# First MLP product of the last three chunks from seven block products instead of eight, on one Trainium2 core

## The chip, the core and the metric

The kernel runs on one core of a Trainium2 chip. The metric is the device time of one execution in microseconds (us), median of the runs of a kernel. The profile names the engines: PE is TensorE (matrix products) and PEld its weight loads, DVE is VectorE, ACT is ScalarE, POOL is GpSimd, SP is SyncE, which issues transfers.

## The reference, cut to what matters

An attention over four batches of 768 rows is followed by a Fourier mixing and a normalised MLP. The change touches the MLP's first product alone.

```
attn = softmax(scores with a global/local mask and a distance bias) @ v     # 4 batches, 8 heads, 768 x 64
x = attn, heads joined                                                      # [4, 768, 512]
u = x + real(fft(fft(x, axis=1), axis=2))
un = (u - mean) / sqrt(var + 1e-06)
out = u + maximum(un @ w_ch1, 0) @ w_ch2                                    # w_ch1 [512, 2048], w_ch2 [2048, 512]
```

## The kernel before, in words

**Tiling.** The MLP works on twelve chunks of 256 rows, three per batch, so that chunks 9, 10 and 11 are those of the last batch. A chunk has two halves of 128 rows. `un` is brought to the layout `UNT[c]` (features on the partitions) by a transposing transfer (`nt_dma`, issued by SP). The first product, `un @ w_ch1`, is made by `ph_unit(c, jp)`, eight units per chunk: a unit is 8 matmuls of 128x128 weights against 256 columns (2 of the 16 blocks of hidden features, 4 blocks of input features each), and one evacuation of a 128x512 PSUM bank with the relu to the tile `hT`, on ACT (L1344) or DVE (L1345). The second product is in `pg_units(c)`. For chunks 2 to 11 it is already made from seven block products in place of eight: units p1, p45, p6, p7, p32, with sums of `hT` blocks made on DVE (`s_sums`: s1, s2, s3, s4) and sums of `w_ch2` blocks made once (`w2_sums`). Each p unit ends in a DVE operation that adds the product, scaled, to `u` (L1502).

**Order.** Nothing is scheduled at run time. Every operation is registered with a name, and `ORDER` lists for each engine the names in the order in which it issues them; each engine works strictly in that order. A planner made the lists from its own costs (functions `mm_us`, `act`, `dve`, `dve2`, `pool`) and a rule for DVE operations that run beside POOL copies (`beside`, `SLOW`). A name is the unit and the operation's number in it: `H72.0` is the first operation behind PE unit H72.

Names that the steps below use:

- PE: `H8c`..`H8c+7` are the units of chunk c's first product. `G` are the units of the second: chunk 6 is G36 to G40, chunk 7 G41 to G45, chunk 8 G46 to G50, chunk 9 G51 to G55, chunk 10 G56 to G60, chunk 11 G61 to G66. `A64` is a score unit and `A73` to `A76` are the four products of the last batch's attention weights with v. M27, M28, M30, M31 are the last batch's Fourier products `py`, M29 and M32 the products `pu` that give u for chunks 9 and 10 (M29) and 11 (M32).
- DVE: T.191 to T.196 are the folds ahead of M27 and M28 (T.191 is L907 and L908). T.220 is s4 of chunk 5; T.224, T.225, T.227 are s1, s2, s3 of chunk 6; T.241 and T.242 are s1 and s2 of chunk 9; T.247 to T.250 belong to chunk 10, T.252 to T.255 to chunk 11. M29.0, M29.6 and M32.0 add `pu` to x for chunks 9, 10 and 11. T.197 is the copy of a mirrored block (L1139 to L1141) that M32 reads.
- POOL: M23.11, M26.5, M29.5 ... are the two small operations (L1285, L1286) that make 1/std of a chunk; T.190 gathers x of the last batch; T.234 and T.251 store chunks 7 and 10 by an indirect transfer (L1355).
- SP: T.189 reads x of the last batch; T.198 to T.200 are the transposing transfers of chunks 9 to 11; T.222 and T.223 store chunk 5, T.228 and T.229 chunk 6, T.239 and T.240 chunk 8, T.256 to T.258 chunk 11 in three pieces.

PSUM has eight banks: two pairs in the ring `xx` (scores, attention products, Fourier products), two banks in `ph`, two in `pg`. The attention weights stand in four tiles `ex0` to `ex3` (`expst`), which the last batch leaves free after A73 to A76.

Of the kernel before, what the change touches and what calls it, by code (L numbers as in the profile page):

```python
# [24 lines left out]
class Plan:  # L25
# [96 lines left out]
    def op_go(self, eng, name, start):  # L122
# [6 lines left out]
        if eng == "POOL":  # L129
            self.ports.append((start, end, 1 if dma else 0 if outs and outs[0][0] in ("vB", "kB") else 2))  # L130
# [23 lines left out]
    SLOW = ((0.56, 1.0, 1.0), (0.38, 0.7, 1.0))  # L154
    ports = ()

    def beside(self, start, cost, kind):

        left, t = cost, start
        names = self.todo["POOL"]  # L160
        ports = self.ports[-3:]
        if names:
            s = self.op_start("POOL", names[-1])
            if s is not None:
                p = self.made[names[-1]]
                ports = ports + [(max(s, start), max(s, start) + p[0]["POOL"][0], 1 if p[7] else 0 if p[3] and p[3][0][0] in ("vB", "kB") else 2)]
        for a, b, dma in ports:
            if b <= t:
                continue
            if a > t:  # L170
                if a - t >= left:
                    break
                left -= a - t
                t = a
            rate = self.SLOW[kind][dma]
            if (b - t) * rate >= left:
                return t + left / rate - start
            left -= (b - t) * rate
            t = b
        return t + left - start  # L180
# [40 lines left out]
    def unit_start(self, unit):  # L221
# [7 lines left out]
        if not there:  # L229
# [33 lines left out]
        ),  # L263
        "DVE": (
# [11 lines left out]
        ),  # L276
        "POOL": (
# [8 lines left out]
            "T.140 T.205 T.212 T.206 T.186 T.211 T.149 T.179 T.180 T.150 T.151 T.229 T.189 T.228 T.223 T.222 T.198 T.199 T.200 T.240 T.239 T.245 T.246 "  # L286
            "T.256 T.258 T.257 "
# [73 lines left out]
def kernel(  # L361
# [986 lines left out]

    GP = {}
# [125 lines left out]
    def pg_units(c):  # L1475
# [104 lines left out]
        PG.append((h0 + wd + [("D",)], ("pg",), p1))  # L1580
        PG.append((h1 + [("s", c, 1)] + ws, ("pg",), p45))
# [31 lines left out]
    with tc.manual_schedule():  # L1613
# [76 lines left out]
        for b in range(B):  # L1690
# [49 lines left out]
            nt_unit(b, 2)  # L1740
        for c in range(NP * B):
            for jp in range(NJ // 2):
                ph_unit(c, jp)
# [7 lines left out]
        for i in range(2):  # L1751
            w2_sums(i)
        pl.run([MIX, ATT, PH, PG])
# [35 lines left out]
```

## Time and profile before

| what | value |
|---|---|
| time, median of 3 runs | 245.82 us (245.44 to 248.03) |
| span of the profiled execution, first to last instruction | 244.1 us |
| median less span (what lies around the span; the profile does not give the execution's own time beside its span) | 1.7 us |
| PE busy | 232.0 us, 95% |
| DVE, ACT, POOL busy | 193.4, 138.8, 114.8 us |

How to read it: an engine's busy time is the union of its instructions. The chain that ended last follows the work back from the last instruction; the line that stands there for a stretch is what set the time in it. A row of the time line gives the start, the duration, the engine, the line of the kernel, and out<-in. Where a row merges several instructions, the duration is that of them all. A PE row ends some 0.17 us after the next one has begun, since matmuls are pipelined; the pace is read from start to start. DVE and ACT rows overlap in the same way by about 0.1 us.

### The profile page before, as it was taken

What the parts mean: (1) busy time and instruction counts of PE and PEld (TensorE: products, weight loads), DVE (VectorE), ACT (ScalarE), POOL (GpSimd) and SP (SyncE); (2) the same over time, 40 slices, a digit from 0 to 9 for tenths busy, and PEclk for the clock granted to TensorE, in tenths of its full rate; (3) what the DMA queues carried; (4) which work ended last, traced back from release to release, by engine and by line L of the source; (5) the groups of instructions that cost most, each with busy time, mean ns of one, the idle gap of its engine ahead of it and who ended that gap; (6) DMA issues with size and microseconds to landing.
All of it is one profiled execution on the core that took longest, in us unless ns stands there. A gap on an engine that the chain in (4) does not pass through costs nothing.

```text
span 244.1 us, 7606 instructions
## 1 busy us (share of the span) xinstructions
PE 232.0 (95%) x3251; PEld 191.2 (78%) x3251; DVE 193.4 (79%) x420; ACT 138.8 (57%) x226; POOL 114.8 (47%) x164
## 2 busy tenths in 40 slices
PE   7679899999999999999999999999999999999993
PEld 2557776878677667788989888898889898888883
DVE  2559997879972789999999889889998755846483
ACT  2368788864657468658357788364534651434200
POOL 8998898866590038999059056500300320011020
PEclk9997999999999999999999999999999999999999
DMA  6999999999999999999999979220570330040212
GB/s 170 181 169 145 157 235 172 197 190 196 110 145 152 234 179 205 117 135 110 242 184 285 135 84 156 46 33 13 174 258 4 77 99 0 1 130 1 89 72 99
DMA packets 95938, 32.85 MB, mean 135 GB/s; under 512 B 84160, under 2 KB 92480, under 8 KB 95904
## 3 DMA queue, kind: packets, MB, share of 16 engines
q0 software_dynamic: 66176, 17.06, 71.7%
q1 hardware_dynamic: 26560, 12.56, 25.1%
q10 hardware_dynamic: 3168, 2.75, 4.1%
q8 instruction: 25, 0.41, 0.7%
q14 instruction: 9, 0.07, 0.1%
HBM read 31.44 MB, written 8.65 MB: 164 GB/s over the span
## 4 chain that ended last, share of the span: by engine, by line
PE 67%; DMA 14%; DVE 5%; ACT 5%; POOL 3%; issue 3%; SPq 1%; POOLq 0%
PE ph L1339 29%; PE pgD L1484 14%; PE pgA L1484 10%; DMA qk<-in_q_dram 4%; DMA v<-in_v_dram 4%; PE py L1105 3%; DMA hT<-in_q_dram 3%; PE pg L1370 3%; PE pav L822 3%; ACT ex L766 2%; DMA back<-backm 2%; DMA xr<-xd,back 2%; PE sc L737 2%; PE pu L1192 1%; ACT mk L1657 1%
## 5 line engine op out<-in xcount | busy, mean ns | idle before, releaser
L1339 PE MATMUL ph<-unT,w 128*128 128x256 f16 x768 | 94.4, 273 | 0.8 <-issue 0.4
L1339 PEld LDWEIGHTS <-w 128*128 128x128 f16 x768 | 73.6, 98 | 12.5 <-issue 1.2
L1344 ACT ACTIVATE hT<-ph 128x512 f16<-128x512 f32 x73 | 42.9, 596 | 54.6 <-PE ph L1339 52.6
L1484 PEld LDWEIGHTS <-hT 128*128 128x128 f16 x320 | 31.0, 98 | 4.3 <-issue 0.4
L1285 POOL TENSOR_SCALAR sm<-sm 128x2 f32<-128x2 f32 x12 | 3.4, 284 | 58.2 <-ACT un L1278 57.8
L763 ACT ACTIVATE er<-sc 128x1024 f16<-128x1024 f32 (+1 forms) x24 | 22.3, 951 | 11.4 <-PE sc L737 8.2
L1345 DVE TENSOR_SCALAR hT<-ph 128x512 f16<-128x512 f32 x23 | 15.7, 687 | 12.7 <-PE ph L1339 12.7
L766 ACT ACTIVATE ex<-sc 128x1024 f16<-128x1024 f32 (+1 forms) x24 | 21.7, 955 | 7.1 <-PE sc L743 6.9
L1502 DVE SCALAR_TENSOR_TENSOR u<-pgA,sm,u 128x256 f32<-128x256 f32 (+1 forms) x30 | 16.9, 568 | 6.4 <-PE pgA L1484 6.0
L1502 DVE SCALAR_TENSOR_TENSOR u<-pgD,sm,u 128x512 f32<-128x512 f32 (+1 forms) x21 | 15.2, 722 | 3.5 <-PE pgD L1484 3.3
L1355 POOL DMA_INDIRECT out_dram<-u,back x4 | 4.5, 1120 | 27.5 <-DVE rev L1140 16.3
L887 POOL DMA_INDIRECT xr<-xd,back x3 | 4.8, 1602 | 25.4 <-PE pg L1370 16.1
L1370 PE MATMUL pg<-w,hT 128*128 128x512 f16 x64 | 16.0, 379 | 0.0
L1118 ACT ACTIVATE zy<-py 128x1024 f16<-128x1024 f32 (+1 forms) x13 | 11.1, 857 | 8.4 <-PE py L1105 6.1
L778 DVE TENSOR_TENSOR ex<-er,mk 128x1024 f16<-128x1024 f16 (+1 forms) x24 | 15.1, 646 | 0.7 <-ACT er L763 0.7
L1278 ACT ACTIVATE un<-un 128x512 f16<-128x512 f16 x24 | 15.0, 625 | 1.1 <-DMA unT<-un 1.1
L552 POOL DMA_DIRECT2D qk<-in_k_dram x16 | 13.7, 903 | 1.2 <-DMA w<-in_moe_w_ch_dram 0.8
L1269 ACT ACTIVATE un<-u,sm 128x512 f16<-128x512 f32 x19 | 13.1, 717 | 1.9 <-DVE sm L1251 0.7
L552 POOL DMA_DIRECT2D qk<-in_q_dram x16 | 13.6, 870 | 0.0
L822 PEld LDWEIGHTS <-ex 128*128 128x128 f16 x352 | 12.4, 97 | 1.1 <-ACT ex L766 0.4
L834 DVE TENSOR_TENSOR x<-pav,rc 128x384 f16<-128x384 f32 x24 | 12.6, 554 | 0.6
L822 PE MATMUL pav<-v,ex 128*128 128x65 f16 x224 | 12.9, 193 | 0.2
(170 smaller groups left out, 492.9 us busy)
## 6 DMA issues: line engine op xcount, KB each, us to landing
w<-in_moe_w_ch_dram POOLq DMA_DIRECT2D x8, 512.0 KB, 13.4
out_dram<-u SPq DMA_DIRECT2D x15, 256.0 KB, 3.0
v<-in_v_dram POOLq DMA_DIRECT2D x12, 192.0 KB, 5.8
qk<-in_k_dram POOLq DMA_DIRECT2D x16, 96.0 KB, 5.4
qk<-in_q_dram POOLq DMA_DIRECT2D x16, 96.0 KB, 4.5
xr<-xd SPq DMA_DIRECT2D x3, 512.0 KB, 4.6
xd<-x ACTq DMA_DIRECT2D x2, 768.0 KB, 4.5
v<-in_v_dram POOLq DMA_DIRECT2D x8, 96.0 KB, 7.0
```

Source lines behind the costliest of these rows:

```text
L552: nc.gpsimd.dma_start(qk16[n][:, w, :, h], src[b, h0 + h].rearrange("(i m) d -> m i d", m=P))
L763: A(mine(), cut(pa), AF.Exp, 0.0, 0.125)
L766: A(cut(expst[hp][:, :, g * 512:g * 512 + (384 if g == 2 else 512)]), cut(pa), AF.Exp, 0.0, 0.125)
L778: VT(o, mine(), m, op=ALU.mult)
L822: nc.tensor.matmul(o[:, s * 65:(s + 1) * 65], lhsT, w, start=(a == 0), stop=(a == len(ops) - 1), skip_group_check=True)
L1278: A(x, x, AF.Square, accum_out=MV[c][:, a, 2:3])
L1339: nc.tensor.matmul(ph[:, a * CH:(a + 1) * CH].rearrange("p (x m) -> p x m", x=2), W1[0][:, d, jb * P:(jb + 1) * P], UNT[c][:, :, d, :], st ...
L1344: pl.later([("ACT", act(512), lambda: A(dst, ph, AF.Relu)), ("DVE", dve(512), lambda: V.tensor_scalar_max(dst, ph, 0.0))], [], e, [("h", c ...
L1345: ("DVE", dve(512), lambda: V.tensor_scalar_max(dst, ph, 0.0))],
L1370: nc.tensor.matmul(pg, HT[c][:, jb, t * P:(t + 1) * P], W2[0][:, jb, :], start=(jb == 0), stop=(jb == NJ - 1))
L1484: nc.tensor.matmul(o, lhs(j), rhs(j), start=(first and j == 0), stop=(j == NK - 1), skip_group_check=True)
L1502: V.scalar_tensor_tensor(o, x, r(t), acc, op0=ALU.mult, op1=ALU.add)
```

## The change

The first product of chunks 9, 10 and 11 is written as a two-by-two block product and made from seven block products in place of eight (the form with 15 additions, of which four are of weights, four of inputs and seven of products).

- **Grouping.** Chunk 9 is by itself: its two halves of 128 rows are the block columns, so its matmuls stream 128 columns. Chunks 10 and 11 are taken together: each is one block column, so their matmuls stream 256 columns. The blocks of `w_ch1` are halves of its input features and of its hidden features.
- **PE.** The 24 units H72 to H95 go. Chunk 9 has 2 parts, chunks 10 and 11 have 4 parts; a part has seven units u0 to u6. New numbers: H72 to H78 and H79 to H85 for chunk 9, H86 to H92, H93 to H99, H100 to H106, H107 to H113 for chunks 10 and 11. A unit is 8 matmuls of 128 columns (chunk 9) or 4 matmuls of 256 columns.
- **PSUM.** A part takes a pair of banks of `xx`. Bank A collects u0, u2, u4, u5, bank X is used by u1, u3 and u6. After u0, u2 and u4 the running sum in A is copied to SBUF as fp32 (`keep`, ACT or DVE); the next product into A waits for that copy. After u1, u3 and u6 DVE adds X and a kept copy to fp16 (`add`), and a relu in place follows on ACT, DVE or POOL. u5's bank A is evacuated with the relu, as before.
- **Sums.** Four sums of weight blocks, 128x2048 fp16 each, T.263 to T.266, on POOL, are written into `ex0` to `ex3` as A73 to A76 leave them free. Four sums of inputs: T.267 to T.270 for chunk 9 (256 wide) and T.271 to T.274 for chunks 10 and 11 (512 wide); T.268, T.270 and T.272 are on POOL, the others on DVE.
- **Order.** The lists are the same up to G36 on PE. T.197 moves from DVE to POOL. T.222 and T.223 move ahead of T.189 on SP, T.240 moves between T.256 and T.258. T.188 (write of x of the last batch) comes earlier on ACT. M27 and M28 come later on PE, M32 earlier. All of chunks 10 and 11's second product (G56 to G66) now follows the last unit of the first (H113). p1 and p45 of chunks 10 and 11 may also use `ph` banks.
- The planner counts POOL's new sums and relus as copies in its rule for DVE (`COPIES`).

The diff, cut to its core (the order lists from where they differ):

```diff
         "PE": (
-  ... H61 G36 H58 H56 G37 H62 G38 H63 H60 G39 H57 G40 G41 H66 H68 M27 H64 G42 M28 H67 G43 M29 M30 H65 G44 M31 H71 G45 H69 H70 G46 H76 H73 M32 H77 G48
-  H79 G47 H72 G50 H75 H74 G49 H78 G51 H84 H80 G52 H81 H86 G53 H85 H82 G55 H83 G54 H87 H92 H89 H94 H91 G56 H95 H90 G57 H93 H88 G58 G59 ... G66
+  ... H61 G36 H56 G37 H57 H63 H60 G38 H62 H58 G39 G40 G41 H70 H66 G42 H68 G43 M27 M28 H69 M30 M29 G44 H67 G45 H64 M31 H65 H71 M32 G46 H72 G47 H74 H73
+  H79 H80 H76 H75 H81 G48 H77 H83 H82 G50 H84 H78 H85 G49 H93 H86 G51 H87 G52 H94 H88 H95 G53 H90 H97 H89 H96 H91 H98 H92 H99 G54 H100 H107 H108 H101
+  H102 H109 G55 H104 H111 H103 H110 H105 H112 H106 H113 G56 G61 G62 G57 G58 G63 G59 G60 G64 G65 G66
         "DVE": (
+  ... A66.1 T.220 A65.1 A76.0 A64.1 G35.0 A75.0 A74.0 T.224 G34.0 T.191 T.225 T.227 G36.0 G37.0 T.192 ... G45.0 M29.6 T.235 T.236 T.267 G46.0 T.269 M32.0
+  ... T.241 G49.0 G51.0 T.242 T.271 T.273 H87.0 T.243 T.274 ... H103.0 H110.0 H103.1 H106.0 T.252 H113.0 H113.1 G56.0 T.247 G61.0 ... G66.0
         "POOL": (
-  ... T.217 T.148 T.175 M23.5 T.173 M23.11 T.190 T.234 M26.5 M29.5 M32.5 M29.11 T.251
+  ... T.217 T.148 T.175 M23.5 T.173 T.263 T.264 M23.11 T.265 T.190 T.197 M26.5 T.266 T.234 M29.5 T.268 T.270 T.272 M29.11 H110.1 M32.5 H106.1 T.251
...
+        def wsum(i):
+            SW[i] = expst[i].rearrange("p s n -> p (s n)")[:, 0:2048].rearrange("p (d f) -> p d f", d=2)
+            return SW[i]
+        steps = ((lambda e: e(wsum(0), a(1, 0), a(1, 1), op=ALU.add), ()), (lambda e: e(wsum(1), SW[0], a(0, 0), op=ALU.subtract), (0,)),
+                 (lambda e: e(wsum(2), a(0, 0), a(1, 0), op=ALU.subtract), ()), (lambda e: e(wsum(3), a(0, 1), SW[1], op=ALU.subtract), (1,)))
+        for i, (fn, on) in enumerate(steps):
+            pl.later([("POOL", pool(2048) + 0.3, lambda fn=fn: fn(nc.gpsimd.tensor_tensor)), ("DVE", dve2(2048), lambda fn=fn: fn(VT))],
+                     [("avh", B - 1, i)] + [("w1", x) for x in range(4)] + [("sw", x) for x in on], 0.0, [("sw", i)], rank=2)
...
+            def prod(o, lhs, rhs, first):
+                for a in range(NF):
+                    for d in range(2):
+                        oo = o[:, a * N:(a + 1) * N]
+                        nc.tensor.matmul(oo.rearrange("p (x m) -> p x m", m=P) if two else oo, lhs(NF * jp + a, d), rhs[:, d],
+                                         start=(first and a == 0 and d == 0), stop=(d == 1), skip_group_check=True)
...
+            def keep(n, e):
+                x = 3 * slot + n
+
+                def cp(on):
+                    if x not in KT:
+                        KT[x] = buf(*HOME[x], [P, 512], FP32, 1)
+                    copy_on(on, KT[x], cell["A"])
...
+            def add(i, k, n, e, ring=None):
+                o, x = at(i, k), cell["X"]
+                pl.later([("DVE", dve(512), lambda: VT(o, bk(x), bk(KT[3 * slot + n]), op=ALU.add))], [("k", n, g, jp)], e, [("hs", g, i, k, jp)],
+                         ring=ring, rank=0)
+                relu(i, k)
...
+            PH.append(([("unT", cs[0])] + wt, (kind,), u0))
+            PH.append(([("unT", cs[0]), ("u0", g, jp)] + free("hT", 2 + cs[0]), (kind,) if kind == "ph" else None, u1))
+            PH.append(([("sw", 1), ("su", g, 1), ("k", 0, g, jp)], None, u2))
+            PH.append(([("sw", 2), ("su", g, 2), ("hs", g, 0, 0, jp)] + (free("zy", 2 * B) if cs[-1] == NP * B - 1 else []), None, u3))
+            PH.append(([("sw", 0), ("su", g, 0), ("k", 1, g, jp)] + (free("zy", 2 * B) if cs[-1] == NP * B - 1 else []), None, u4))
+            PH.append(([("sw", 3), ("unT", cs[-1]), ("k", 2, g, jp)], None, u5))
+            PH.append(([("su", g, 3), ("hs", g, 1, 1, jp)], None, u6))
```

More of the change, by code (lines that the diff above doesn't have):

```diff
@@ L129, in op_go @@
         if eng == "POOL":
-            self.ports.append((start, end, 1 if dma else 0 if outs and outs[0][0] in ("vB", "kB") else 2))
+            self.ports.append((start, end, 1 if dma else 0 if outs and outs[0][0] in self.COPIES else 2))
         if dma:
@@ L154 @@
     SLOW = ((0.56, 1.0, 1.0), (0.38, 0.7, 1.0))
+    COPIES = ("vB", "kB", "sw", "su", "h", "ht")
     ports = ()
@@ L165, in beside @@
                 p = self.made[names[-1]]
-                ports = ports + [(max(s, start), max(s, start) + p[0]["POOL"][0], 1 if p[7] else 0 if p[3] and p[3][0][0] in ("vB", "kB") else 2)]
+                ports = ports + [(max(s, start), max(s, start) + p[0]["POOL"][0], 1 if p[7] else 0 if p[3] and p[3][0][0] in self.COPIES else 2)]
         for a, b, dma in ports:
@@ L285 @@
             "T.6 T.0 T.9 T.136 T.35 T.127 T.133 T.128 G7.1 T.134 T.91 G3.1 T.10 T.137 T.130 T.100 T.131 T.101 T.102 T.176 T.182 T.177 T.34 T.185 T.183 "
-            "T.140 T.205 T.212 T.206 T.186 T.211 T.149 T.179 T.180 T.150 T.151 T.229 T.189 T.228 T.223 T.222 T.198 T.199 T.200 T.240 T.239 T.245 T.246 "
-            "T.256 T.258 T.257 "
+            "T.140 T.205 T.212 T.206 T.186 T.211 T.149 T.179 T.180 T.150 T.151 T.222 T.223 T.189 T.229 T.228 T.198 T.199 T.200 T.245 T.239 T.246 T.256 "
+            "T.240 T.258 T.257 "
         ),
@@ L1347, in ph_unit, with weight_sums, a @@
         PH.append((needs, ("ph",), run))
+    GW = ((9,), (10, 11))
+    KIND = (("xx", "xx"), ("xx", "xx", "xx", "xx"))
+    SW = {}
+    KT = {}
+    SUM_AT = (("x", 3), ("eA", IA(B - 1, NA(B - 1)) + 1))
+    HOME = [("qk", 10 + x) for x in range(4)] + [("qkT", HP * B + x) for x in range(2)]
+    def weight_sums():
+        def a(i, j):
+            return W1[0][:, 2 * j:2 * j + 2, i * 1024:(i + 1) * 1024]
+        def wsum(i):
[6 more added lines that the diff above has]
+                     [("avh", B - 1, i)] + [("w1", x) for x in range(4)] + [("sw", x) for x in on], 0.0, [("sw", i)], rank=2)
@@ L1579, in pg_units @@
         wd = [("w2", a) for a in range(4)]
-        PG.append((h0 + wd + [("D",)], ("pg",), p1))
-        PG.append((h1 + [("s", c, 1)] + ws, ("pg",), p45))
+        PG.append((h0 + wd + [("D",)], ("pg", "ph") if c >= NP * B - 2 else ("pg",), p1))
+        PG.append((h1 + [("s", c, 1)] + ws, ("pg", "ph") if c >= NP * B - 2 else ("pg",), p45))
         PG.append(([("s", c, 2), ("ra", c, 0)] + ws, None, p6))
@@ L1740 @@
             nt_unit(b, 2)
+        seven = []
         for c in range(NP * B):
-            for jp in range(NJ // 2):
-                ph_unit(c, jp)
+            if not any(c in cs for cs in GW):
+                for jp in range(NJ // 2):
+                    ph_unit(c, jp)
+            for g, cs in enumerate(GW):
+                if c == cs[0]:
+                    seven.append(Seven(g))
+                    for jp in range(8 // seven[g].NF):
+                        seven[g].part(jp)
             if c >= CS:
@@ L1752 @@
             w2_sums(i)
+        weight_sums()
+        for x in seven:
+            x.sums()
         pl.run([MIX, ATT, PH, PG])
```

101 lines of the change are left out of this document (added), and 58 rows, old and new, of the table ORDER.

## Prediction

> **What bounds the kernel now.** I read the page first (its span is below), then the busy times by stretch, then the chain that ended last, then the groups by line, and last the time line around the places where the change puts work. A measurement of this kernel can tell about 1% from no change, 2.46 us of the 245.82 us median.
>
> ```profile
> span 244.1 us, 7606 instructions
> ...
> L1339 PEld LDWEIGHTS <-w 128*128 128x128 f16 x768 | 73.6, 98 | 12.5 <-issue 1.2
> ```
>
> ```profile
> core 0: us, PE busy (x) PEld busy (x) DVE busy (x) ACT busy (x) POOL busy (x), PEclk, DMA share, GB/s
> 200.00:240.00 40.00, 40.00 (x366) 35.61 (x365) 25.72 (x45) 11.52 (x22) 3.14 (x5) 1.00 0.14 47
> 160.00:180.00 20.00, 20.00 (x217) 18.06 (x215) 18.73 (x35) 9.60 (x21) 2.10 (x3) 1.00 0.39 106
> ```
>
> ```profile
> 160.17 1.75 PE pgD L1484 x16
> ...
> 163.46 0.67 PE pav L822 x22
> ...
> 165.87 0.87 PE pgA L1484 x8
> ...
> 196.46 0.89 PE pu L1192 x16
> ...
> 220.06 4.37 PE ph L1339 x40
> ...
> 233.16 1.88 PE pgA L1484 x16
> ...
> 237.65 1.00 PE pgD L1484 x8
> ```
>
> In the second view, PE is busy all the time from 160 to 180 and from 200 to 240 us at the full granted clock (PEclk 1.00), and in the third, the chain, it stands in every line of this stretch (the chain's starts of PE lie 0.17 us behind the time line's). So PE bounds the part that the change touches: a matmul less is its time less, and a PE wait is a wait of the whole. Beside it DVE has 14.3 of 40 us to spare from 200 to 240 us and ACT 28.5, but from 160 to 180 us DVE works 18.73 of 20 us.
>
> **PE's work.** 40 matmuls of 256 columns take 4.37 us, 109.2 ns each; 16 of 128 columns, each with its own weights, take 0.89 us, 55.6 ns each. The units that go: 24 x 8 x 109.2 ns = 20.97 us. Those that come: chunk 9, 2 x 7 x 8 = 112 x 55.6 ns = 6.23 us; chunks 10 and 11, 4 x 7 x 4 = 112 x 109.2 ns = 12.23 us. Gain 2.51 us. [...]
>
> Two PE waits at the end go as well: 16 matmuls at 233.16 took 1.88 us for 1.75, and 8 at 237.65 took 1.00 for 0.87, 0.26 us together. The new end order (G56 G61 G62 G57 ...) leaves each unit's operand ready before its turn by the durations below, closest G63, which waits for T.253 with 0.17 us to spare.
>
> **Evacuations.** A part has three copies, three additions, three relus and one relu out of PSUM where there were four relus out of PSUM.
>
> ```profile
> L1344 ACT ACTIVATE hT<-ph 128x512 f16<-128x512 f32 x73 | 42.9, 596 | 54.6 <-PE ph L1339 52.6 <-issue 1.9
> ```
>
> ```profile
> L1345 DVE TENSOR_SCALAR hT<-ph 128x512 f16<-128x512 f32 x23 | 15.7, 687 | 12.7 <-PE ph L1339 12.7
> ...
> L1232 DVE SCALAR_TENSOR_TENSOR u<-pu,xr 128x512 f32<-128x512 f32 x12 | 7.8, 686 | 1.4 <-PE sc L737 0.8 <-PE pu L1192 0.5
> ...
> L920 DVE TENSOR_SCALAR zy<-ww 128x512 f16<-128x512 f16 x6 | 1.5, 290 | 0.0
> ```
>
> The groups of ACT, then those of DVE: copy 0.60 us on ACT or 0.69 on DVE, addition 0.69 (a PSUM and an SBUF operand, as in L1232; bounds 0.69 and 0.75, the row at 233.20 below), relu in place 0.29 on DVE (L920) or 0.60 on ACT, 0.45 in the mean. Six parts: 18 x (0.60 + 0.69 + 0.45) + 6 x 0.60 = 35 us against 24 x 0.62 (596 and 687 ns, mixed 73 to 23) = 15 us, 20 us more on ACT and DVE. The 42.8 us that they have to spare from 200 to 240 us cover it; without them it would cost all 20.
>
> What could cost is the chain inside a part. The hops are read from these rows of the time line: G59 ends as G60 begins (233.00), DVE starts 0.20 us later, and G61 starts 0.05 us after DVE's end.
>
> ```profile
> 233.00 1.04 PE L1484 MATMUL pgA<-misc,hT 128*128 128x256 f16 x8
> 233.20 0.75 DVE L1502 SCALAR_TENSOR_TENSOR u<-pgD,sm,u 128x512 f32<-128x512 f32 x1 [0.31 <-PE pgD L1484]
> 234.00 1.03 PE L1484 MATMUL pgA<-w,hT 128*128 128x256 f16 x8
> ...
> 235.11 1.24 POOL L1355 DMA_INDIRECT out_dram<-u,back  x1 [10.01 <-DVE u L1502]
> ...
> 237.69 0.48 DVE L1502 SCALAR_TENSOR_TENSOR u<-pgA,sm,u 128x256 f32<-128x256 f32 x1
> ...
> 240.95 0.33 SPq L1597 DMA_DIRECT2D out_dram<-u  x1
> ```
>
> So u0 to u2 needs 0.20 + 0.60 + 0.05 = 0.85 us over ACT. Two parts are interleaved: between H104 and H105 stand H111, H103 and H110, 1.31 us. Laying the durations end to end in the written order of each engine from A64 on, I find every such link ready in time; the smallest margins are 0.1 us (H99, H100, H113). Cost nothing, at most 0.5 us if each hop is 0.05 us longer and the addition 0.75.
>
> **Sums of weights on POOL.** This is the unknown: no row shows a wide two-operand operation on POOL. The time line of POOL, then that of DVE:
>
> ```profile
> 148.71 0.41 POOL L1140 COPY rev<-zy 128x254 f16<-128x254 f16 x1
> 149.05 0.88 POOL L1141 COPY rev<-zy 128x256 f16<-128x256 f16 x1
> ...
> 152.52 1.13 POOL L795 COPY vB<-v 32x528 f16<-32x528 f16 x1
> 153.74 0.51 POOL L1285 TENSOR_SCALAR sm<-sm 128x2 f32<-128x2 f32 x1
> 154.33 0.73 POOL L1286 TENSOR_TENSOR sm<-sm,mhalf 128x2 f32<-128x2 f32 x1
> ...
> 155.71 0.62 POOL L795 COPY vB<-v 32x528 f16<-32x528 f16 x1
> ```
>
> ```profile
> 148.76 0.92 DVE L1451 TENSOR_TENSOR hT<-hT 128x1024 f16<-128x1024 f16 x1
> 149.60 0.74 DVE L778 TENSOR_TENSOR ex<-er,mk 128x768 f16<-128x768 f16 x1
> ...
> 158.01 0.55 DVE L778 TENSOR_TENSOR ex<-er,mk 128x768 f16<-128x768 f16 x1
> 158.47 0.69 DVE L1459 TENSOR_TENSOR sb<-hT,sb 128x1024 f16<-128x1024 f16 x1
> ...
> 168.34 0.95 DVE L907 TENSOR_TENSOR eA<-x 128x1536 f16<-128x1536 f16 x1
> 169.21 0.95 DVE L908 TENSOR_TENSOR eA<-x 128x1536 f16<-128x1536 f16 x1
> ...
> 188.94 0.85 DVE L1244 SCALAR_TENSOR_TENSOR u<-pu,xr 128x384 f32<-128x384 f32 x1
> ...
> 190.87 0.16 DVE L1248 TENSOR_TENSOR u<-pu,xr 128x1 f32<-128x1 f32 x1
> ```
>
> Below: a copy of 528 takes 0.62 us (155.71), so 2048 take 2.4. Above: twice that, 4.7, for two operands, or because a POOL copy beside a busy DVE took 1.13 us for 0.62. I take 4.7, since DVE is at 94% where the sums run. (512 wide: 0.6 to 1.2 us.) [...]
>
> The other way round, L1451 took 0.92 us for 0.69 (L1459's shape) beside the two POOL copies (0.24 us of the 0.84 from its start to the next one's), and L778 0.74 for 0.55 with 0.33 us of overlap: DVE went at 0.71 and 0.42 of its pace. I take 0.56, between them; the ends stay for the range.
>
> T.263 runs from 156.3 us (POOL is free at the end of L795 at 155.71) to 161.0. A DVE operation takes 0.08 us less from start to start than it lasts (L907, L908). Beside T.263, A66.1 (L778, 0.46 us start to start) and T.220 (L1459, 0.61) take 1.9 us for 1.07, and G35 (160.17 in the chain), which waits for T.220 with 0.8 us to spare, comes 0.04 us late. A74 (163.46 in the chain) ends at 163.96, so T.264 runs from 164.2 to 168.9, then M23.11 for 1.0 us (0.51 + 0.73 at 153.74, less what DVE adds there), then T.265 from 169.9 to 174.6. On DVE's path to G38 stand T.224, T.225, T.227 (0.60 each), T.191 (1.9), G34.0 (0.67) and G36.0 (0.48). Alone they end at 170.2; G38's turn is seven blocks of 0.873 us (G36, H56, two for G37, H57, H63, H60) after G36's start (165.87 in the chain, 165.71), 171.82. With the 0.5 us that DVE is behind after T.263, and 0.56 of the pace beside the sums: T.224 ends at 166.95, G34.0 at 167.62, T.191 at 170.1, T.225 at 171.15, T.227 at 172.2, G36.0 at 172.7: G38 is 0.9 us late. T.192 behind it is slowed as well, and G39 loses 0.2, M28 0.06 us.
>
> **The other moves.** M32 waits for a bank that M29.6 reads, now closer behind M29: PE has 6.33 us of work between them, DVE begins M29.6 0.20 + 0.67 us after G45's end, at 4.36, and reads the bank for 2.1 (L1244 at 188.94 to L1248's end): 0.2 us late. H88 waits for T.272: from G51's end DVE needs 0.20 + 0.40 + 0.60 (T.242) + 0.42 (T.271), POOL 1.2, hops 0.1, together 2.9 us, and PE has H87, G52 and H94, 2.62: 0.3 us late; at 0.6 us on POOL none. T.197 on POOL takes 1.2 us for its two larger copies (L1140, L1141 above), and M26.5, T.266, T.234, M29.5 and T.268 queue behind it; H74 needs T.268 last and has 0.2 us left. T.222 and T.223 are ready before T.189, nothing waits. T.240 holds SP's queue 0.4 us at the end, while PE is on G65 and G66. T.251 starts 1.0 us after G60's end (0.20 + 0.75 + 0.05) and the last store 3.35 after it (2.62 for G64 to G66, 0.20 + 0.48 + 0.05), so 2.35 us apart in place of 5.8. Its landing takes 3.7 us against 1.7, and it still comes 0.35 us ahead:
>
> ```profile
> DMA to landing us min/median/max: 3.5/3.7/5.5
> ```
>
> ```profile
> DMA to landing us min/median/max: 1.7/1.7/1.8
> ```
>
> (the first of L1355, the second of L1597). Cost 0 to 0.7 us; I take nothing.
>
> **Sum.** -2.51 - 0.26 + 0.04 + 0.9 + 0.2 + 0.06 + 0.2 + 0.3 = -1.07 us. Against the profiled span, 244.1 - 1.07 = 243.0; with the 1.7 us between span and median, 245.82 - 1.07 = 244.8 us.
>
> **Rivals.**
> - *The sums disturb nobody.* At 2.4 us and any pace down to 0.56 no place on DVE's path is late, and only M32's 0.2 us remains: -2.56, 243.3 us. For it: a copy of 528 that takes 0.62 us. Against: DVE's load there.
> - *Slower: the sums hold DVE.* One mechanism, at G38. DVE has 1.6 us to spare there; each further us of DVE lateness is a us of PE. At 4.7 us and a pace of 0.42, G35 is 0.7 and G38 1.9 us late, the sum is +0.3 us, 246.1. At 5.5 us G38 is 2.3 us late, G39 0.4, and T.268 comes late for H74 by 0.5: +2.1, 247.9. From 5.7 us on, it is slower by over 1%. For it: the 0.42 of L778. Against: the 0.71 of L1451.
> - *128 columns are paced by their weight loads.* A load lasts 98 ns (PEld, the page's row). Were it not hidden behind a matmul of half the length, chunk 9's 112 matmuls would cost 10.98 us in place of 6.23: +4.75 on the forecast, 249.5 us. The 16 matmuls with 16 loads in 0.89 us are against it.
> - *The change does not do what it says*: seven products but more columns. The count above excludes it.
>
> **How the numbers follow.** Forecast 0.52, alone between 243.8 and 245.7 us (no hop longer, a pace of 0.5 to 0.7). Sums disturb nobody 0.24, half of it below 243.36, the 1% bound. Sums hold DVE 0.22, of which 0.13 over 248.28 and 0.09 within. Weight loads 0.02, over. So faster 0.12, same 0.52 + 0.12 + 0.09 = 0.73, slower 0.15. The range from 243.2 to 248.2 us leaves out 0.05 below and 0.15 above.
>
> **What would show it.** Right: 112 matmuls each of 55.6 and 109.2 ns; T.263 to T.266 at 4 to 5 us; PE waits at G38 behind DVE u L1502, at M32 and at H88 behind POOL; no wait above 0.1 us inside the parts. Wrong: sums under 3 us (then 243.3), DVE two-operand rows over 1.5 us beside them (then 246 or more), PE waits on copies or additions, or a last store that lands after 244 us.

## The result, and the profile after

The changed kernel takes 267.0 us (median of 4 runs, 264.5 to 268.3) against 246.9 us of the kernel before in the same comparison: a ratio of 1.080, 95% interval 1.071 to 1.089. The prediction was 244.8 us, at most 248.2 us. The profiled span went from 244.1 to 262.5 us. Times here and below are medians of all executions of a kernel; the ratios leave out the executions that took over 1.5% more than its fastest, which matters most for e10 (four of twelve). The page of the kernel after begins:

```profile
span 262.5 us, 7752 instructions
...
PE 233.8 (89%) x3283; PEld 190.1 (72%) x3283; DVE 213.0 (81%) x442; ACT 145.1 (55%) x240; POOL 138.4 (53%) x176
```

The busy times by stretch of the kernel after, for the two stretches that the prediction showed of the kernel before:

```profile
core 0: us, PE busy (x) PEld busy (x) DVE busy (x) ACT busy (x) POOL busy (x), PEclk, DMA share, GB/s
160.00:180.00 20.00, 14.67 (x162) 12.89 (x162) 19.66 (x26) 9.12 (x19) 11.58 (x6) 0.99 0.39 114
200.00:240.00 40.00, 36.08 (x371) 30.66 (x369) 29.26 (x64) 24.56 (x50) 8.20 (x9) 1.00 0.20 54
```

PE, which had been busy for all of both stretches, now idles 5.3 of the 20 us and 3.9 of the 40. DVE is busy for 19.66 of 20 us, but with 26 instructions where there were 35. What PE waited for from 150 us on (engine, line, releaser: total in us, times, longest):

```profile
PE ph L1344 <- DVE hT L1350: 2.7, 1, 2.7
PE pgA L1660 <- DVE u L1678: 2.7, 1, 2.7
PE pgD L1660 <- DVE u L1678: 1.9, 1, 1.9
PE phA L1425 <- ACT zy L1503: 1.8, 4, 0.6
PE phA L1425 <- DVE hT L1464: 1.0, 3, 0.5
PE pgA L1660 <- DVE mk L1630: 0.8, 1, 0.8
PE phA L1425 <- ACT qk L602: 0.7, 2, 0.5
```

Three long waits for DVE ahead of 180 us (PE units H50, G37 and G38), then many short ones at the seven-product matmuls (L1425). POOL's time line, then DVE's, at the three long ones:

```profile
156.04 4.04 POOL L1369 TENSOR_TENSOR ex<-w 128x2048 f16<-128x2048 f16 x1
166.70 4.06 POOL L1369 TENSOR_TENSOR ex<-ex,w 128x2048 f16<-128x2048 f16 x1 [6.62 <-PE pav L827]
...
172.11 4.64 POOL L1370 TENSOR_TENSOR ex<-w 128x2048 f16<-128x2048 f16 x1
```

```profile
156.69 3.42 DVE L1241 TENSOR_SCALAR sm<-sm 128x2 f32<-128x2 f32 x1
160.03 0.68 DVE L1350 TENSOR_SCALAR hT<-ph 128x512 f16<-128x512 f32 x1
...
167.87 3.44 DVE L1624 TENSOR_TENSOR eg<-hT 128x1024 f16<-128x1024 f16 x1
...
171.89 0.94 DVE L912 TENSOR_TENSOR eA<-x 128x1536 f16<-128x1536 f16 x1
172.75 4.80 DVE L913 TENSOR_TENSOR eA<-x 128x1536 f16<-128x1536 f16 x1
```

An operation on two columns lasts 3.42 us, and L913 4.80 us where its twin L912 took 0.94. The first two end within 0.6 us of POOL's sum (160.08 and 170.76), L913, which still has most of its own 0.95 us to do, 0.8 us behind it (176.75). That is no slower pace: DVE stands until the sum is over, and then needs little less than the operation's own time (0.55 us of 0.68 for L1624, 0.80 of 0.95 for L913). The relu behind L1241 (L1350 at 160.03) frees the bank that PE waits for. And the granted clock:

```profile
176.00:179.20 3.20, 0.55 (x6) 0.34 (x4) 3.20 (x5) 1.51 (x4) 2.36 (x2) 1.00 0.00 0
...
180.00:182.00 2.00, 2.00 (x11) 1.44 (x10) 2.00 (x5) 0.00 (x0) 0.00 (x0) 0.50 0.12 47
...
183.00:186.00 3.00, 3.00 (x29) 2.69 (x28) 1.52 (x4) 1.09 (x2) 0.00 (x0) 1.00 0.00 0
```

Behind the third gap PE gets half the clock (0.50) from 179.5 to 183.0 us: 16 matmuls that start 0.213 us apart and not 0.109.

**A ledger.** The table comes from the starts of successive matmuls in each trace. A step of over 0.25 us is a gap and counts with what it has above the usual 0.109 us (a gap named in the text is the whole step, 0.11 us longer); steps of 0.15 to 0.235 us are taken as half clock and count in the same way, though a few short waits fall under them too (0.05 to 0.26 us where the clock stood at 1.00); the rest is PE's time for the matmuls themselves. It begins at the last score matmul (`sc`), because the part ahead of it differs from one execution to the next (that matmul starts at 157.8 to 162.1 us in these profiles). All in us.

| kernel | gaps before the parts | in the parts | in the end | half clock | matmuls alone | last matmul to end | total |
|---|---|---|---|---|---|---|---|
| before | 0 | - | 0 | 0.05 | 81.99 | 3.96 | 86.0 |
| after | 7.71 | 7.37 | 0.92 | 1.85 | 79.61 | 7.25 | 104.7 |
| e1 cut sums | 0 | 7.40 | 0.92 | 0.25 | 79.55 | 7.25 | 95.4 |
| e2 two tiles | 7.70 | 0.65 | 1.20 | 3.14 | 79.52 | 7.25 | 99.5 |
| e3 before, with sums | 7.24 | - | 0 | 1.64 | 82.01 | 3.96 | 94.8 |
| e4 sums on DVE | 0.81 | 9.96 | 0.92 | 0.26 | 80.82 | 7.25 | 100.0 |
| e5 cut sums, two tiles, end | 0 | 0.47 | 0.63 | 0.05 | 79.26 | 5.60 | 86.0 |
| e6 end | 7.83 | 7.36 | 0.18 | 1.78 | 79.60 | 5.61 | 102.4 |
| e7 sums in pieces | 5.23 | 7.80 | 0.92 | 2.94 | 79.74 | 7.25 | 103.9 |
| e8 mended | 0 | 1.77 | 0.63 | 0.09 | 79.37 | 5.61 | 87.5 |
| e9 before, with copies | 1.33 | - | 0 | 0 | 82.02 | 3.96 | 87.3 |
| e10 mended, 2nd | 1.18 | 0.65 | 1.85 | 0.05 | 79.36 | 3.96 | 87.0 |
| e11 mended, 3rd | 3.19 | 0.47 | 0.51 | 1.84 | 79.39 | 3.96 | 89.3 |
| e12 mended, 4th | 0 | 1.13 | 0.51 | 0.21 | 79.47 | 4.07 | 85.4 |

After against before: 2.4 us fewer for the matmuls, as planned, and 21.1 us lost: 7.7 in the three gaps, 1.8 at half clock, 7.4 inside the parts, 0.9 in the end, 3.3 behind the last matmul. (Line numbers move by a few between kernels: L1241 is L1236 before and in some versions, L1425 is L1421 or L1426.)

### The profile page after: what moved, and what is told of

It reads as the page before. It is cut to its first block, busy times and chain, and to the rows that moved or that the text cites. A ratio compares the mean times of both kernels' runs of the same rounds, so it can differ in the third digit from the quotient of the medians.

```text
span 262.5 us, 7752 instructions
## 1 busy us (share of the span) xinstructions
PE 233.8 (89%) x3283; PEld 190.1 (72%) x3283; DVE 213.0 (81%) x442; ACT 145.1 (55%) x240; POOL 138.4 (53%) x176
## 4 chain that ended last, share of the span: by engine, by line
PE 61%; DVE 20%; ACT 5%; DMA 5%; issue 4%; POOL 2%; ACTq 0%; DVEq 0%; POOLq 0%
PE ph L1344 19%; PE pgD L1660 9%; PE pgA L1660 6%; PE pg L1546 5%; PE phA L1425 4%; PE py L1110 4%; PE pav L827 3%; DMA u<-in_k_dram 2%; PE pu L1197 2%; ACT ex L771 2%; DVE eA L913 2%; PE sc L742 2%; PE pt L657 2%; DVE eg L1624 2%; PE pf L1018 1%
## 5 line engine op out<-in xcount | busy, mean ns | idle before, releaser
L1344 PE MATMUL ph<-unT,w 128*128 128x256 f16 x576 | 72.3, 276 | 3.6 <-DVE hT L1350 2.7
L1344 PEld LDWEIGHTS <-w 128*128 128x128 f16 x576 | 55.6, 99 | 13.8 <-issue 3.9
L1349 ACT ACTIVATE hT<-ph 128x512 f16<-128x512 f32 x56 | 32.6, 596 | 42.1 <-PE ph L1344 38.7
L1660 PEld LDWEIGHTS <-hT 128*128 128x128 f16 x288 | 27.7, 98 | 5.8 <-issue 2.5
L1350 DVE TENSOR_SCALAR hT<-ph 128x512 f16<-128x512 f32 x16 | 10.9, 684 | 7.5 <-PE ph L1344 7.5
L1290 POOL TENSOR_SCALAR sm<-sm 128x2 f32<-128x2 f32 x12 | 5.0, 419 | 17.9 <-ACT un L1283 17.3
L1425 PEld LDWEIGHTS <-ex 128*128 128x128 f16 x128 | 10.1, 97 | 5.4 <-issue 4.4
L827 PEld LDWEIGHTS <-ex 128*128 128x128 f16 x352 | 12.6, 97 | 2.0 <-issue 1.2
L1274 ACT ACTIVATE un<-u,sm 128x512 f16<-128x512 f32 x16 | 11.1, 717 | 3.2 <-DVE sm L1241 2.6
```

The costliest lines, as they stand in the source:

```text
L827: nc.tensor.matmul(o[:, s * 65:(s + 1) * 65], lhsT, w, start=(a == 0), stop=(a == len(ops) - 1), skip_group_check=True)
L1344: nc.tensor.matmul(ph[:, a * CH:(a + 1) * CH].rearrange("p (x m) -> p x m", x=2), W1[0][:, d, jb * P:(jb + 1) * P], UNT[c][:, :, d, :], st ...
L1349: pl.later([("ACT", act(512), lambda: A(dst, ph, AF.Relu)), ("DVE", dve(512), lambda: V.tensor_scalar_max(dst, ph, 0.0))], [], e, [("h", c ...
L1425: nc.tensor.matmul(oo.rearrange("p (x m) -> p x m", m=P) if two else oo, lhs(NF * jp + a, d), rhs[:, d], start=(first and a == 0 and d == ...
L1660: nc.tensor.matmul(o, lhs(j), rhs(j), start=(first and j == 0), stop=(j == NK - 1), skip_group_check=True)
```

## The experiments

Theory HOLD: a sum on POOL stops DVE. Theory PAIR: the two accumulator banks of a part wait for each other because they are one tile. Theory END: the new end order itself. Rivals stand in the expectations.

**e1, the weight sums cut to 16 columns.**

```diff
-            return W1[0][:, 2 * j:2 * j + 2, i * 1024:(i + 1) * 1024]
+            return W1[0][:, 2 * j:2 * j + 2, i * 1024:i * 1024 + 8]
...
-            return SW[i]
+            return SW[i][:, :, 0:8]
```

> The four weight sums on POOL are cut from 2048 columns to 16 (the products then read what the tiles hold: part of the computation is left out); everything else is the changed kernel. Theory HOLD: a two-tile sum on POOL stops VectorE for its whole length, and the three TensorE gaps of the changed profile ahead of 180 us (2.92, 2.18 and 2.94 us, 7.7 us over the normal step) and the lower clock behind them (80 matmuls in 180 to 190 us where there were 102, some 2.1 us) are its price: the span falls from 262.5 to about 252.7 us. Rival ORDER: VectorE is late there because the new order gives it more to do, and the sums are beside it by chance: the gaps stay, and the span stays within 1.5 us of 262.5.

257.0 us, ratio to before 1.042 (1.032 to 1.053), against 1.080. The three gaps are gone, the clock stays at 1.00 from 150 us to the last matmul, and PE is busy for all of 160 to 180 us:

```profile
160.00:180.00 20.00, 20.00 (x232) 17.98 (x217) 17.82 (x35) 10.23 (x21) 3.42 (x5) 1.00 0.53 133
```

L1241 takes 0.17 us again. The order of the work is the same, so ORDER falls and HOLD stands, at 9.3 us in the ledger; the gaps in the parts did not move (7.40). The span, 255.3 us, is 2.6 us above the one expected; 2.1 of them lie ahead of the last score matmul, which starts at 160.0 us here and at 157.8 in the kernel after.

**e2, the two accumulators as two tiles.**

```diff
-                    cell["A"], cell["X"], cell["Xr"] = t[:, 0], t[:, 1], ring
+                    cell["A"] = t[:, 0]
...
-            PH.append(([...] + free("hT", 2 + cs[0]), (kind,) if kind == "ph" else None, u1))
+            PH.append(([...] + free("hT", 2 + cs[0]), ("ph",), u1))
```

> The two accumulators of a seven-product part, which were the two banks of one tile, become two tiles (the second one in a bank of the hidden-layer ring); nothing else differs from the changed kernel. Theory PAIR: the instructions that touch one bank wait for those that touched the other, because both are one tile, and most of the 8.3 us of TensorE gaps between 207 and 249 us come from that: 4 to 7 us of them go, the span falls to 255.5 to 258.5 us. Rival CHAIN: copy, add and relu are too slow by themselves for the steps of TensorE: at most 1.5 us go.

261.4 us, ratio 1.062 (1.049 to 1.075). In the kernel after, three rows of PE, two of ACT and one of DVE from the last two parts show the wait (the time lines of the three engines):

```profile
239.23 1.03 PE L1425 MATMUL phA<-unT,ex 128*128 128x256 f16 x8 [0.36 <-DVE zy L1464]
240.52 0.60 PE L1425 MATMUL phA<-eA,w 128*128 128x256 f16 x4 [0.25 <-ACT zy L1503]
241.75 0.60 PE L1425 MATMUL phA<-eA,w 128*128 128x256 f16 x4 [0.63 <-ACT zy L1503]
```

```profile
239.87 0.60 ACT L1503 ACTIVATE zy<-phA 128x512 f16<-128x512 f32 x1 [1.13 <-PE phA L1425]
241.10 0.60 ACT L1503 ACTIVATE zy<-phA 128x512 f16<-128x512 f32 x1 [0.63 <-DVE zy L1464]
```

```profile
240.37 0.69 DVE L1464 TENSOR_TENSOR zy<-phA,qkT 128x512 f16<-128x512 f32 x1 [1.19 <-PE phA L1425]
```

The rows at 240.52 and 241.75 are H106 and H113 (u6), which write bank X. Each begins 0.05 us after L1503, the relu of u5, has ended, and that reads bank A. DVE's addition at 240.37 reads bank X of H110, whose matmuls were over before 239.2, and waits for H112 in bank A. So instructions on one bank wait for reads of the other: the pair is one tile in the program, and it is guarded as one. (e2 also takes its second bank from another ring, so the run alone does not tell the tile from the ring; these rows do.) The same matmul groups (busy us, mean ns, idle time ahead of them), after and in e2:

```profile
L1425 PE MATMUL phA<-eA,w 128*128 128x256 f16 x16 | 2.4, 271 | 1.8 <-ACT zy L1503 1.8
```

```profile
L1426 PE MATMUL phX<-eA,w 128*128 128x256 f16 x16 | 2.1, 272 | 0.0
```

PAIR holds: of 7.4 us inside the parts 6.7 go. The total fell by 5.2 us only, since this execution had two stretches of half clock at its three gaps (3.14 us against 1.85) and 0.3 us more of gaps in the end.

**e3, the kernel before with the four sums added.**

```diff
-  T.173 M23.11 T.190 T.234 M26.5 M29.5
+  T.173 T.263 T.264 M23.11 T.265 T.190 T.234 M26.5 T.266 M29.5
+        weight_sums()
```

> The kernel before, with the four weight sums of 2048 columns added on POOL at the places of the changed order; nobody reads them. HOLD: the gaps of the changed profile come up in the kernel before too: 6 to 10 us more than its 244.1 us. The prediction's pace of 0.56 beside the sums: 1.1 us more. Sums that disturb nobody: no change.

257.1 us, ratio 1.047 (1.035 to 1.060), 8.8 us in the ledger. Nothing of the seven-product form is in this kernel, and the sums alone make three gaps of 2.92, 2.04 and 2.60 us. DVE's rows:

```profile
158.61 3.43 DVE L1236 TENSOR_SCALAR sm<-sm 128x2 f32<-128x2 f32 x1
161.95 0.68 DVE L1345 TENSOR_SCALAR hT<-ph 128x512 f16<-128x512 f32 x1
...
183.18 4.69 DVE L1061 TENSOR_TENSOR eA<-zy 128x1536 f16<-128x1536 f16 x1
```

**e4, the sums on DVE.** T.263 to T.266 stand behind G43.0, G44.0, G45.0 and G46.0 in DVE's list.

> The changed kernel with its four weight sums moved from POOL to VectorE's list (behind G43, G44, G45 and G46), where one should take about 1.28 us (twice the 0.68 us of a sum of 1024 columns, less the fixed part), 5.1 us in all. HOLD: the gaps ahead of 180 us go as with the cut sums; of the 5.1 us between none and all falls on the path: span 252.7 to 257.8 us. Rival ORDER: VectorE is the bound there, and 5.1 us more of work makes it later still: 262 to 268 us.

261.4 us, ratio 1.060 (1.050 to 1.070). The early gaps fall to 0.81 us, but four sums close together (1.22 us each, the last 1.52) make DVE late for the first part (a gap of 2.15 us at 201.6 us in the matmul starts), and from 203.3 to 206.8 us PE runs at half clock. There its matmuls of 128 columns start 0.107 us apart and not 0.056, which the ledger's bounds do not catch: 1.3 us of the matmuls alone. In all it is 4.7 us more than e1, and the span, 259.8 us, lies above HOLD's range and below ORDER's. The place was bad, as e8 shows.

**e7, the sums in pieces of 512 columns.**

```diff
+        def pieces(o, x, y, op):
+            for d in range(2):
+                for f in range(0, 1024, 512):
+                    nc.gpsimd.tensor_tensor(o[:, d, f:f + 512], x[:, d, f:f + 512], y[:, d, f:f + 512], op=op)
```

> The changed kernel with each weight sum on POOL cut into four instructions of 512 columns (about 1.2 us each as the input sums of 512 columns took). Theory HOLD, one instruction at a time: VectorE gets in between the pieces, no hold is longer than 1.3 us, the gaps of 2.2 to 2.9 us become shorter ones that the two accumulator banks partly cover, and the clock stays at 1.00: span 254 to 259 us. Rival: VectorE is kept out as long as POOL has such work in its queue: the three gaps stay, 262 to 266 us.

264.9 us, ratio 1.072 (1.065 to 1.080), span 263.6 us, within the rival's range: 0.8 us less in the ledger. POOL and DVE in one time line:

```profile
157.95 4.47 POOL L1369 TENSOR_TENSOR ex<-w 128x512 f16<-128x512 f16 x4
...
158.60 3.85 DVE L1241 TENSOR_SCALAR sm<-sm 128x2 f32<-128x2 f32 x1
...
171.41 5.65 POOL L1369 TENSOR_TENSOR ex<-ex,w 128x512 f16<-128x512 f16 x4 [8.99 <-PE pav L827]
...
172.94 1.28 DVE L1629 TENSOR_TENSOR eg<-hT 128x1024 f16<-128x1024 f16 x1
...
174.81 1.25 DVE L912 TENSOR_TENSOR eA<-x 128x1536 f16<-128x1536 f16 x1
...
175.98 1.91 DVE L913 TENSOR_TENSOR eA<-x 128x1536 f16<-128x1536 f16 x1
```

Both theories are half right. Beside the first sum DVE did not get in between the four pieces (3.85 us, to the end of the last); beside the second it did, with 0.3 to 1 us of hold each. The first gap grew to 3.35 us, and half clock cost 2.9 us. Why the first case differs stays open; its operation is the only one of the four with one source and two fp32 columns.

**e9, the kernel before with copies in place of sums.**

```diff
-        steps = ((lambda e: e(wsum(0), a(1, 0), a(1, 1), op=ALU.add), ()), ...
+        steps = ((lambda e: e(wsum(0), a(1, 0)), ()), ...
...
-  lambda fn=fn: fn(nc.gpsimd.tensor_tensor)
+  lambda fn=fn: fn(nc.gpsimd.tensor_copy)
```

> The kernel before with four copies of 2048 columns on POOL (one source, some 2.1 to 2.6 us each by the 0.62 to 0.67 us of copies of 512 and 528) in the places of the four sums (two sources); nobody reads them. The prediction took the pace of VectorE beside such copies, 0.42 to 0.71, for the sums. Theory TWO SOURCES: beside a copy VectorE's two-tile operations go on at that pace, none lasts over twice its usual time, the gaps of TensorE are absent or under 1 us, the span is 244 to 246.5 us. Rival ANY: a copy holds VectorE just as a sum does, for its own length of about 2.2 us; three holds of 1.5 to 2 us give gaps of about half of those of the sums and the span is 247 to 250 us.

249.4 us, ratio 1.013 (1.004 to 1.022). A copy takes 1.89 us, and DVE stands beside it too:

```profile
157.54 1.89 POOL L1359 COPY ex<-w 128x2048 f16<-128x2048 f16 x1
...
177.22 2.36 POOL L1360 COPY ex<-w 128x2048 f16<-128x2048 f16 x1
```

```profile
158.19 1.26 DVE L1236 TENSOR_SCALAR sm<-sm 128x2 f32<-128x2 f32 x1
...
177.74 2.38 DVE L934 SCALAR_TENSOR_TENSOR zy<-ww,eA 128x512 f16<-128x512 f16 x1
```

L1236 ends as the copy does (159.45 and 159.43), L934 0.54 us after it. So it is not the second source of the sum: by these rows ANY holds. The gaps are 0.75 us at most, because the copies are short; the span, 246.7 us, lies between the two ranges.

**e6, the end in another order.**

```diff
-  PE   ... H113 G56 G61 G62 G57 G58 G63 G59 G60 G64 G65 G66
+  PE   ... H113 G56 G61 G57 G62 G58 G59 G60 G63 G64 G65 G66
-  POOL ... M29.11 H110.1 M32.5 H106.1 T.251
+  POOL ... M29.11 M32.5 T.251        (H110.1, H106.1 at the end of ACT's list)
-  SP   ... T.245 T.239 T.246 T.256 T.240 T.258 T.257
+  SP   ... T.245 T.240 T.239 T.246 T.256 T.258 T.257
```

> The changed kernel with the end alone put in another order: the relus H106.1 and H110.1 on ScalarE and not on POOL, G57 to G60 ahead of G62 to G66, the old store of chunk 8 ahead in SyncE's queue. Theory END: the 1.03 us gap at 248 us goes, and the time from the last matmul to the end falls from 7.2 us to about 4.0 as before, since POOL's store of chunk 10, behind whose landing SyncE's last stores wait, starts earlier: 3 to 4.2 us less, a span of 258 to 259.5 us. Rival: the stores at the end only follow VectorE's last sums, and 1 us at most goes.

DVE's list follows the new order too. 264.6 us, ratio 1.072 (1.065 to 1.079). The gap falls to 0.18 us in the ledger and the time behind the last matmul to 5.61 us: 2.4 us, less than expected, but by the expected cause. In the kernel after, SP's queue had its longest single wait for POOL's indirect store; below that wait stand the store's row on POOL and SP's first store behind it:

```profile
SPq L1773 <- DMA out_dram<-u,back: 20.2, 1, 20.2
```

```profile
254.14 1.07 POOL L1531 DMA_INDIRECT out_dram<-u,back  x1 [8.44 <-DVE u L1678]
...
257.62 0.33 SPq L1773 DMA_DIRECT2D out_dram<-u  x1
```

SP's store comes 3.5 us after POOL's, whose landings take 3.4 to 5.6 us in this trace. In e6 the two stand at 254.86 and 258.33 us, again 3.5 us apart, but POOL's is now 2.1 us and not 1.2 us ahead of the last matmul.

**e5, all three causes taken away.** The edits of e1, e2 and e6 together; as in e1, part of the weight sums is left out.

> Three edits together: the weight sums cut to 16 columns (part of the computation is left out), the two accumulators as two tiles, and the end put in another order (the two relus of POOL on ScalarE, the last units of chunk 10 ahead of those of chunk 11, the old store of chunk 8 ahead in SyncE's queue). Theory LEDGER: the 18.4 us that the changed kernel lost in its profiled span are 7.7 us of gaps and 2.1 us of lower clock from the sums, 8.3 us of gaps in the seven-product parts, 3.2 us more between the last matmul and the end, less 2.9 us of columns; with all three causes gone the span is 241 to 245 us. Rival HIDDEN: behind the three lies another bound (VectorE's list, copies of ScalarE): 247 us or more.

247.9 us, ratio 1.003 (1.000 to 1.007). The profiled span is 244.6 us, within LEDGER's range; the other nine are 244.8 to 247.3 us, so by the span the two theories are told apart only narrowly, and the ledger, with no gap over 0.6 us, speaks for the first. Even with sums that cost nothing the kernel is no faster than before: the matmuls save 2.7 us, 1.1 us of gaps stay, and the end is 1.6 us longer, because chunks 10 and 11 now finish together and POOL's store with its landing comes later.

**e8, e10, e11, e12: complete versions.** All have e2's tiles and e6's edits. The weight sums stand as follows, and from e10 on all of chunk 10's units stand ahead of G62 (the end of DVE's list follows).

```diff
  e8    DVE: T.192 T.263 ... T.193 T.264 ... T.238 T.265;  POOL: T.266
  e10   DVE: T.192 T.263 ... T.193 T.264 ... T.195 T.266;  POOL: T.265;  PE: G56 G61 G57 G58 G59 G60 G62 G63 G64 G65 G66
  e11   DVE: T.192 T.263 ... T.193 T.264 ... T.233 T.266;  G57.0 ahead of T.250, T.254 ahead of G62.0
  e12   as e11, with M29.2 on ACT and not on DVE
```

> A complete version: accumulators as two tiles, the end in the other order, three of the weight sums on VectorE where it was idle with cut sums (behind T.192, T.193 and T.238: idle 0.97, 0.46 and 0.57 us), the fourth on POOL where it held nothing up. LEDGER: as the run with cut sums in this same form, plus 1.8 us (3 x 1.28 less 2.0 us of idle time): 243 to 247 us, about as before. Rival: VectorE, busy 9 of 10 us from 150 to 200, hands the 3.8 us on to TensorE in full, and more where the gaps lower its clock: 248 to 252 us.

250.3 us, ratio 1.013 (1.006 to 1.020). Two sums on DVE in places where it had idled make no gap; the third makes one of 1.23 us at 203.3 us, and the span, 248.8 us, lies in the rival's range.

> The complete version once more, with two places changed: the third sum on POOL beside VectorE's run of PSUM operations and the fourth on VectorE behind T.195 (before, the third stood between the accumulators' first add and its chain, and TensorE had a gap of 1.23 us there), and in the end all of chunk 10's units but G61 ahead of G62, so that POOL's store starts earlier. Theory LEDGER: from the last score matmul to the end, 87.5 us in the version before it, 0.5 to 1 us less from the gap and 1.0 to 1.6 us less at the end: 85 to 86 us, against 86.0 us of the kernel before, a ratio of 0.99 to 1.00. Rival: the c10-first order makes TensorE wait for VectorE's block sums by as much as the end gains: 87 to 88 us.

249.1 us, ratio 1.004 (1.000 to 1.008). The time behind the last matmul is that of before (3.96 us), as LEDGER has it, but DVE's sums leave gaps of 1.28 us at 186 and of 1.22 and 0.84 us in the end, as the rival has it: 87.0 us in the ledger.

> The version before it with VectorE's list mended at the three places where TensorE waited: the fourth weight sum behind T.233 instead of T.195 (a gap of 1.28 us at 186 us), G57.0 ahead of T.250 and T.254 ahead of G62.0 and T.255 (gaps of 1.22 and 0.84 us in the end). LEDGER: 87.0 us from the last score matmul to the end, less 0.9 to 1.2 us, less some 1.2 us: 84.6 to 85.3 us, against 86.0 us of the kernel before, a ratio of 0.99 to 1.00. Rival: VectorE has no room left in these places, and the gaps move to the next wait instead of going: 86.5 to 87.5 us.

250.2 us, ratio 1.013 (1.008 to 1.017). The two gaps in the end fall to one of 0.62, but a new one of 3.29 us comes up at 194 us, with half clock behind it: 89.3 us in the ledger, outside both ranges. POOL and DVE:

```profile
192.05 4.04 POOL L1366 TENSOR_TENSOR ex<-w 128x2048 f16<-128x2048 f16 x1
...
192.18 4.20 DVE L1271 TENSOR_SCALAR un<-u,sm 128x512 f16<-128x512 f32 x1
```

DVE, a sum later than before, reaches L1271 0.13 us after POOL has begun, and stands for the whole sum. In e8 it had been 0.6 us ahead of it.

> The version before it with one operation moved: the centring of one half of a chunk (M29.2, a VectorE operation with one SBUF source, usually 0.49 us) goes to ScalarE. In the version before it POOL's sum had started 0.13 us ahead of it, and it took 4.20 us; TensorE's gap of 3.29 us at 194 us and the 1.84 us of lower clock behind it came from there. HOLD: with no operation on VectorE that reads SBUF alone during that sum, both go: 89.3 less 3.2 less 1.8 = 84.3 us from the last score matmul to the end, 85.5 at most if ScalarE's 0.7 us more delay a relu, against 86.0 us before. Rival: VectorE is late there for the sum on its own list in any case, and a gap of 1 us or more stays: 85.5 to 87 us.

247.2 us, ratio 0.998 (0.995 to 1.002). With this half of L1271's work on ACT nothing on DVE reads SBUF alone during the sum, and every row beside it has its usual length. Three of them:

```profile
191.56 0.68 DVE L1345 TENSOR_SCALAR hT<-ph 128x512 f16<-128x512 f32 x1
192.16 0.74 DVE L1673 SCALAR_TENSOR_TENSOR u<-pgA,sm,u 128x512 f32<-128x512 f32 x1
...
193.48 0.85 DVE L1244 SCALAR_TENSOR_TENSOR u<-pu,xr 128x384 f32<-128x384 f32 x1
```

The ledger has 85.4 us, 0.6 under before. One operation moved was worth 3.0 us of time (250.2 to 247.2). It is the best version, and it does not beat the kernel before by anything that can be measured.

## Why the prediction was wrong, point by point

- **Matmul columns, -2.51 us, and the two short waits at the end, -0.26 us: right.** Both lie in the ledger's column of the matmuls alone (waits of 0.13 us are under its bound), which fell by 2.2 to 2.7 us in every version but e4 (half clock stands in that column there). Eight matmuls of 128 columns take 0.45 us from start to start in e5's chain, some 56 ns each as forecast, so the rival of the weight loads is out.
- **Size of the sums, 4.7 us: within its bounds, 0.6 us too long.** Undisturbed they took 4.04 to 4.07 us; the 4.64 of the third includes a wait of its own.
- **The pace of 0.56: the step that failed most.** It was read from DVE rows beside POOL copies of 0.4 to 0.9 us as a slower pace. The same rows fit a hold: POOL's copy at 148.71 ended at 149.12, and L1451, begun at 148.76, ended 0.56 us after that; the copy at 149.05 ended at 149.93, and L778, begun at 149.60, ended 0.41 us after that. Each is 0.13 or 0.14 us less than the operation's own 0.69 and 0.55, and behind the sums L1624 and L913 end in the same way (0.13 and 0.15 us less). An average over short POOL instructions looks like a pace; over one of 4 us it is 2.8 to 3.9 us of standing still. It cost 7.7 us of gaps and 1.8 us of clock where the sum had 1.2 us (G35 to M28). The rival "the sums hold DVE" had the right name and the wrong mechanism; its last priced case, 247.9 us, was still a pace. G38 was named rightly as a place; H50 (behind L1241, of two columns) and G37 (behind L1624) were not named. The prediction's own sign of being wrong, two-operand DVE rows over 1.5 us, came up at once (3.44 and 4.80).
- **The clock: not in the prediction.** In the trace before it stood at 1.00 from 21.2 us to the last matmul (at 0.50 from 17.8 to 21.2); that it falls to 0.50 behind a gap of PE's own, as from 179.5 to 183.0 us in the kernel after, was not priced.
- **Evacuation chains, nothing to 0.5 us: wrong by 7.4 us,** though every duration was right (copy 0.594, addition 0.686). The chains were laid out by bank; the program guards the tile. With one tile for each bank 0.65 us is left, near the bound given.
- **The new end order, no wait but 0.17 us to spare at G63, and the last store, 0 to 0.7 us: wrong.** G63 waited 0.92 us (POOL's two relus took 1.50 us each, which the prediction had not priced, and s1 of chunk 10 waited for one), and 3.3 us came behind the last matmul. The text compared landing times; in fact SP does not issue its store before POOL's has landed (3.5 us apart in both traces above). The waits of SP in the trace before show that already:

```profile
SPq L1597 <- DMA out_dram<-u,back: 11.7, 1, 11.7
```

- M32 and H88, 0.5 us together: H88 waited 0.28 us for POOL (222.96), near the 0.3; no wait at M32 was seen.

Together: the sum had -1.07 us and the ledger has +18.7. Of the 19.8 us between them the pace has 8.3 (9.5 with the clock, for 1.2), the chains 7.4, the end 4.2, and the columns and short waits 0.4; the 0.5 us of M32 and H88 go off again.

## What to carry to other kernels

Before putting work on GpSimd, look at what VectorE runs beside it: in these runs an operation there with its sources all in SBUF stood until GpSimd's sum or copy of 2048 columns was over, even one of two columns (3.42 us for 0.17 in the kernel after), and one that reads PSUM went on (0.68 to 0.85 us as usual in e12). When two accumulators take turns, give each a tile of its own, and read the waits of the built program and not only the data flow. And when an engine with no slack feeds the bound, price a long instruction by the longest stop that it can cause, and look for the wait in every queue that an order edit passes.

## What the runs showed of the hardware

- **VectorE beside GpSimd.** Held for the whole rest of a POOL sum or copy of 2048 columns: L1241 (one fp32 source, 0.17 us, took 3.42), L1271 (0.49, 4.20), L1624, L913, L1061 and L934 (SBUF sources, 0.68 to 0.96, took 2.38 to 4.80). Not held: all with a PSUM source (in e12 0.68, 0.74 and 0.85 as usual). The other way round POOL's third sum took 4.64 us for 4.04, having begun at 172.11 while L912 ran (171.89 to 172.83). Why the one engine stands for the other these runs do not show.

  Beside POOL's own operations of two columns no VectorE operation was held: in the traces before and after none that lay beside them and beside no sum was over 0.04 us longer than usual (L1454, 0.72 us at 153.48 in before, for 0.68). In the kernel after, L1276, the operation that took 4.20 us in e11, has its usual length, and all of it lies beside one of these:

```profile
198.15 0.48 DVE L1276 TENSOR_SCALAR un<-u,sm 128x512 f16<-128x512 f32 x1
```

```profile
198.01 0.72 POOL L1291 TENSOR_TENSOR sm<-sm,mhalf 128x2 f32<-128x2 f32 x1
```

  So not every POOL row holds VectorE for all of its length; whether a short one does for a part of it, these runs do not show.
- **Half clock.** After a gap of 2.94 us PE ran at a granted clock of 0.50 for 3.41 us (179.5 to 183.0), 1.8 us lost. Between 150 us and the last matmul the granted clock of stretches of 10 us (what it lacks of 1.00, times 20 us) gives the same 3.4 us in e2 (0.83 from 160 to 170 us, and again from 180 to 190), e3 (0.94 and 0.89 from 180 to 200), e4 (0.83 from 200 to 210) and e6 (0.83 from 180 to 190), and 6.8 us in e7 (0.66 from 160 to 170). Each began in or right behind a gap of 2.15 us (e4) to 3.35 us (e7). How many of the three gaps brought one differed: one in the kernel after, two in e2; why, these runs do not show.
